# A third staging buffer for q and k, q's scale in its split, and a longer load in the planner of an attention and gated-MLP kernel

## The chip, the cores and the metric

The kernel runs on one core of a Trainium2 chip. The metric is the device time of one launch in microseconds (us): 979.78 us is the median of three runs of the kernel before (976.35 to 979.81). Traces are of one profiled execution; its span is 979.5 us.

The core has five engines with a queue each, which run in order and wait for one another by semaphores: TensorE (PE; its weight loads, PEld, are listed apart), VectorE (DVE), ScalarE (ACT), GpSimd (POOL) and SyncE (SP), which only issues DMAs here.

## The reference

Attention with rotary embedding over 8 batches x 8 heads, 576 positions, 64 features a head, and then a gated MLP on the heads put side by side (512 features). Cut to what matters:

```python
q_rot, k_rot = rotate(q), rotate(k)                # x1*cos - x2*sin, x1*sin + x2*cos
scores = scale * q_rot @ k_rot.T                   # scale = 1/sqrt(64) = 0.125
attn = softmax(scores)
x = (attn @ v).transpose(0, 2, 1, 3).reshape(8, 576, 512)
h = relu(x @ w_in);  u, v = halves of h            # 1024 -> 512 + 512
v_n = (v - mean(v)) / sqrt(var(v) + 1e-6)
v_s = einsum("ts,bsd->btd", w_spatial, v_n) + b_spatial
out = (u * v_s) @ w_out
```

## The kernel before, in words

**Tiling.** The 64 heads are worked off as 32 pairs, `i` = 0 to 31, four pairs a batch; a pair fills the 128 partitions. The two heads of a pair are called 0 and 1, and each has five row tiles of 128 (the last of 64) against all 576 keys: the score tiles (0,0) to (0,3), one tile (0,4) that both heads share, and (1,0) to (1,3), nine a pair. Behind the fourth pair of each batch stands that batch's MLP. Its matmuls are spread over the four pairs that come next.

**Precision.** Most matmuls run on operands that are split in two: a rounded part "hi" (made by ACT, `round_hi`, L309) and the remainder "lo" = x - hi (`rest_lo`, L312, on DVE or POOL). The products hi.hi, hi.lo and lo.hi are added up.

**Preparing a pair** (`prepare(i)`). Two tiles `st{i}_0` (q) and `st{i}_1` (k), each 128 x 1216 floats, are loaded with 576 KB each (all loads are issued by SyncE, L306). Each tile holds x and x with its halves swapped. Two products with the tables of cosines and sines (L401) and a sum (L405) make the rotation; for q the table is `tabq`, the table `tabs` times 0.125, made once by ACT (L465). Then ACT rounds q into the second half of its tile, q's remainder overwrites the sum (L312), ACT rounds k (L309, two instructions), and k's remainder goes to `lk`. Ten DMAs stack the parts into `qs0`, `qs1`, `ks0`, `ks1` and `qz`, of which there is one set: `ks1` is written again only when the last score tile of the pair before has read it. The slots of `st` come from the pool `stage`, which has two. They go back when the tile's last reader is done: for k these are `lk` and the DMAs to `ks1`.

**A pair's attention.** `scores`: matmuls into PSUM (L536; L546 for pair 0), row maximum (`nmx`, DVE L557), exponential (`e1`, `e2`, ACT L559). `values`: transposes into PSUM slots `tp` (PE L576), their rounding `eh` (ACT L587) and remainder `el` (DVE L312), the product with v (PE L600), an ACT copy `avt` (L617) and a DVE sum into `x32` (L615); then POOL multiplies with the inverse row sums (L710), and ACT and POOL split the result. Pairs 0 to 3 take a simpler path for the values.

**The MLP.** Products `pa` (L744), `pb` (L767, copied out of PSUM by ACT into `u`, L770), `pc` (L785), `pd` (L800, copied out by ACT into `ob`, L803). `tp`, `pa`, `pb`, `pc` and `pd` share three PSUM slots, pool `pm`. A copy out of `pb` or `pd` that comes late holds back the next transposes.

**What sets the order.** All instructions are handed to a list scheduler (`Program.run`), which plays the kernel through with costs and latencies of its own and gives each engine, when it is free, the ready instruction with the lowest key. What comes out is fixed: an engine's queue then runs in just that order on the chip. Its numbers are the costs (`op(DMA, 1640, ...)` for a load of q or k), `LATENCY` (1700 ns behind a DMA), `SLOTS` and the keys. An instruction with `port=True` isn't started by the scheduler while the other of DVE and POOL holds one such. `pair_op` lets the scheduler choose between DVE and POOL for keys under `EARLY` = 140 (up to pair 7) and takes POOL behind that. In the start-up (to about 147 us) DVE also decodes the 64-bit weights (L344 to L353).

Of the kernel before, what the change touches and what calls it, by code (L numbers as in the profile page):

```python
# [9 lines left out]
F32 = mybir.dt.float32  # L10
# [22 lines left out]
SLOTS = {  # L33
    "stage": 2, "lk": 1, "vraw": 2, "vs": 2, "e2": 4, "e1": 2, "eh": 7, "rb": 1, "x32": 1, "xg": 7, "m": 4,
    "small": 3, "nmx": 3, "rt": 2, "sc": 2, "pv": 1, "pm": 3,
# [63 lines left out]
class Op:  # L99
    def __init__(self, costs, key, f, new, port):  # L100
        self.costs, self.key, self.f, self.new, self.port = costs, key, f, new, port
        self.eng = None
        self.waits, self.after, self.bufs = 0, [], []


class Program:
# [4 lines left out]

    def op(self, eng, ns, key, f, r=(), w=(), new=(), port=False):
        return self.either({eng: ns}, key, lambda e: f(), r, w, new, port)

    def either(self, costs, key, f, r=(), w=(), new=(), port=True):

        o = Op(costs, key, f, new, port)
        before = dict.fromkeys(self.writer[t] for t in (*r, *w) if t in self.writer)
        for t in w:
            before.update(dict.fromkeys(self.readers.pop(t, ())))  # L120
        for t in r:
# [12 lines left out]
        self.ops.append(o)
        return o

    def run(self, make):
# [29 lines left out]
        while events:  # L167
# [55 lines left out]
def tile_attention_gated_mlp(  # L223
# [157 lines left out]
    def prepare(i):  # L381
# [13 lines left out]

        def lo_q(e):
            rest_lo(e, st[0][:, :S].bitcast(F32R), st[0][:, :S], hi(0))

        def rope(j, part, eng):
            cols = slice(S * part.start, S * part.stop)  # L400
            f = lambda e: e.tensor_tensor(out=st[j][:, cols], in0=st[j][:, cols], in1=(tabs if j else tabq)[:, cols], op=ALU.mult)  # L401
            pair_op(S * (part.stop - part.start), key - K_ROPE, f, first=eng, r=["tabs" if j else "tabq"], w=[(st[j], c) for c in range(part.start, part.stop)])

# [40 lines left out]
    def prepare_whole(i, b, hp, key):  # L444
# [13 lines left out]

        if i == 0:
            for part in range(2):  # L460
                cols = slice(S * part, S * part + S)
                op(DMA, 820, -70 + part, lambda part=part, cols=cols: load(k[:, cols], qk[b, hp, 1, :, part]), w=[(k, part)], new=[] if part else [k])
                op(DMA, 820, -70 + part, lambda part=part, cols=cols: load(tabs[:, cols], tab[:, part]), w=[("tabs", part)])
            op(DMA, 1640, -68, lambda: load(q.tile, qk[b, hp, 0].rearrange("p c n -> p (c n)")), w=[q], new=[q])
            op(ACT, 1053, -50, lambda: nc.scalar.activation(tabq, tabs, AF.Copy, scale=0.125), r=[("tabs", 0), ("tabs", 1)], w=["tabq", "tabs"])  # L465
            for part in range(2):
                op(DVE, 680, -60, lambda part=part: nc.vector.tensor_tensor(out=turn(k, part, slice(0, S)), in0=turn(k, part, slice(0, S)), in1=turn(tabs, part, slice(0, S)), op=ALU.mult), r=[("tabs", part)], w=[(k, part)], port=True)
            op(DVE, 830, -59, lambda: sum_k(nc.vector), r=[(k, 0), (k, 1)], w=[kf], new=[kf], port=True)
            for n, (c0, c1) in enumerate(((0, Q0), (Q0, S))):
                cols = slice(c0, c1)  # L470
                op(DVE, dve_ns(2 * (c1 - c0)), -58 + 2 * n, lambda cols=cols: nc.vector.scalar_tensor_tensor(out=c2(q.tile)[:, :, cols], in0=c2(q.tile)[:, :, cols], scalar=0.125, in1=c2(tabs)[:, :, cols], op0=ALU.mult, op1=ALU.mult), r=[q, ("tabs", 0), ("tabs", 1)], w=[(q, n)], port=True)
                op(DVE, dve_ns(c1 - c0), -57 + 2 * n, lambda cols=cols: nc.vector.tensor_tensor(out=turn(q, 0, cols), in0=turn(q, 0, cols), in1=turn(q, 1, cols), op=ALU.add), w=[(q, n)], port=True)
        else:
            for j, st in enumerate((q, k)):
                t = ("tabq", "tabs")[j]
                op(DMA, 1640, key - K_LOAD, lambda j=j, st=st: load(st.tile, qk[b, hp, j].rearrange("p c n -> p (c n)")), w=[(st, 0), (st, 1)], new=[st])
                for part in range(2):
                    pair_op(S, key - K_ROPE, lambda e, st=st, part=part, t=(tabq, tabs)[j]: e.tensor_tensor(out=turn(st, part, slice(0, S)), in0=turn(st, part, slice(0, S)), in1=turn(t, part, slice(0, S)), op=ALU.mult), r=[t], w=[(st, part)])
            pair_op(S, key - K_SUM, lambda e: e.tensor_tensor(out=q[:, :S], in0=q[:, :S], in1=q[:, S:], op=ALU.add), r=[(q, 1)], w=[(q, 0)])
            pair_op(S + TW, key - K_SUM, sum_k, pieces=2, r=[(k, 0), (k, 1)], w=[kf], new=[kf])  # L480
        op(DMA, 910, key - K_LOAD + 1, lambda: load(vr.tile, v[b, hp]), w=[vr], new=[vr])
# [452 lines left out]
```

## Time and profile before

| what | us |
|---|---|
| median of three runs | 979.78 (976.35 to 979.81) |
| span of the profiled execution | 979.5 |
| PE busy | 933.2 |
| ACT busy | 736.7 |
| DVE busy | 667.2 |
| POOL busy | 580.7 |
| wait for the first score matmul (L546) on q's products | 10.7 |

The page lists for each group of instructions its line, engine, what it writes and reads, count, busy time and the mean duration of one, and then the idle time of the engine ahead of it with what ended it. In a timeline the columns are start, length, engine, line, and in brackets the engine's idle time before and its releaser. The granted clock of TensorE is 1.00 in every window, so nothing here is a matter of clocks.

### The profile page before, as it was taken

The page shows a single profiled execution, that of the slowest core. Times are in us where ns is not written, and L with a number is a line of the kernel's source. Part 1 is how long each engine was busy: PE and PEld are TensorE (multiplying, and loading weights), DVE is VectorE, ACT ScalarE, POOL GpSimd, SP SyncE. Part 2 cuts the span into 40 slices and gives each one's busy share as a digit, 9 for nine tenths or more (in the row PEclk, how much of TensorE's full clock was granted, in tenths as well). Part 3 has the DMA queues.
Part 4 walks back from the last instruction along what each step waited for, and adds up shares of the span by engine and source line. Part 5 has one row for each costly group of instructions (what it writes and reads, how often), then busy time and mean ns, then how long its engine had stood idle before and what let it go on. Part 6 is the DMA issues. An engine that isn't in the chain of part 4 may idle for free.

```text
span 979.5 us, 19484 instructions
## 1 busy us (share of the span) xinstructions
PE 933.2 (95%) x6614; PEld 853.3 (87%) x6614; DVE 667.2 (68%) x1479; ACT 736.7 (75%) x1839; POOL 580.7 (59%) x505
## 2 busy tenths in 40 slices
PE   4988999999999999999999999999999999999998
PEld 2555689998899989999899988999889988999998
DVE  5899897766867577675776658676676756767331
ACT  4788798677976779776897768877797677976452
POOL 5566356656757656774756756666585765672121
PEclk9999999999999999999999999999999999999999
DMA  7776644454254554445444444445524455330101
GB/s 264 236 233 170 180 117 118 126 150 126 82 139 114 155 150 109 106 119 161 126 124 117 113 147 125 119 126 150 142 78 125 125 152 149 97 91 21 61 1 49
DMA packets 56181, 124.64 MB, mean 127 GB/s; under 512 B 13201, under 2 KB 13201, under 8 KB 56082
## 3 DMA queue, kind: packets, MB, share of 16 engines
q1 hardware_dynamic: 56082, 123.40, 45.7%
q8 instruction: 53, 0.87, 0.3%
q14 instruction: 46, 0.38, 0.1%
HBM read 66.03 MB, written 9.58 MB: 77 GB/s over the span
## 4 chain that ended last, share of the span: by engine, by line
PE 61%; ACT 13%; DMA 10%; DVE 7%; POOL 5%; issue 2%; SPq 2%; ACTq 0%; POOLq 0%; DVEq 0%
PE pc L785 12%; PE sc L536 10%; PE tp L576 9%; PE pv L600 9%; PE pd L800 7%; PE pb L767 6%; PE pa L744 4%; ACT e L559 4%; POOL st L401 3%; DMA st<-in_qk_dram 3%; DMA qs<-st 3%; DVE nmx L557 2%; SPq L306 2%; ACT eh L587 2%; ACT vv L827 2%
## 5 line engine op out<-in xcount | busy, mean ns | idle before, releaser
L587 ACT ACTIVATE eh<-tp 128x384 fp32r<-128x384 f32 (+1 forms) x504 | 217.5, 433 | 87.8 <-PE tp L576 70.6
L312 DVE TENSOR_TENSOR el<-tp,eh 128x384 fp32r<-128x384 f32 x336 | 185.8, 554 | 107.5 <-ACT eh L587 98.2
L559 ACT ACTIVATE e<-sc,nmx 128x576 f32<-128x576 f32 x288 | 213.0, 741 | 37.0 <-DVE nmx L557 34.1
L557 DVE TENSOR_REDUCE nmx<-sc 128x1 f32<-128x576 f32 x288 | 214.9, 748 | 31.9 <-PE sc L536 23.3
L576 PE MATMUL tp<-ident,e 128*128 128x128 f32 (+1 forms) x1176 | 196.9, 273 | 16.1 <-ACT ob L803 9.3
L401 POOL TENSOR_TENSOR st<-st,tabq 128x576 f32<-128x576 f32 x60 | 85.1, 1435 | 167.6 <-DMA st<-in_qk_dram 105.9
L576 PEld LDWEIGHTS tp<-ident,e 128*128 128x128 f32 (+1 forms) x1176 | 144.8, 138 | 34.2 <-ACT ob L803 10.7
L600 PE MATMUL pv<-eh,vs 128*128 128x384 f32 (+1 forms) x560 | 154.0, 316 | 0.2
L785 PE MATMUL pc<-wsp,vn 128*128 128x288 f32 x768 | 143.2, 303 | 0.5 <-DVE u L843 0.5
L767 PE MATMUL pb<-x,wi 128*128 128x288 f32 x768 | 141.3, 306 | 0.3 <-ACT u L770 0.3
L800 PE MATMUL pd<-g,wo 128*128 128x288 f32 x768 | 140.9, 304 | 0.0
L536 PE MATMUL sc<-ks,qs 128*128 128x288 f32 x620 | 133.1, 304 | 2.8 <-ACT e L559 2.2
L744 PE MATMUL pa<-wi,x 128*128 128x512 f32 x448 | 133.1, 407 | 1.3 <-DVE el L312 1.2
L536 PE MATMUL sc<-lk,qz 128*128 128x288 f32 x558 | 119.6, 296 | 0.0
L785 PEld LDWEIGHTS pc<-wsp,vn 128*128 128x128 f32 x768 | 114.9, 189 | 2.9 <-DVE u L843 0.9
L800 PEld LDWEIGHTS pd<-g,wo 128*128 128x128 f32 x768 | 113.7, 189 | 2.6
L767 PEld LDWEIGHTS pb<-x,wi 128*128 128x128 f32 x768 | 111.9, 189 | 3.3 <-PE pb L767 1.3
L600 PE MATMUL pv<-el,vs 128*64 128x384 f32 (+1 forms) x448 | 113.7, 294 | 0.0
L536 PEld LDWEIGHTS sc<-ks,qs 128*128 128x128 f32 x620 | 99.5, 189 | 13.5 <-ACT e L559 7.1
L312 DVE TENSOR_TENSOR eh<-tp,eh 64x256 fp32r<-64x256 f32 (+1 forms) x168 | 59.7, 356 | 65.2 <-ACT eh L587 56.8
L600 PEld LDWEIGHTS pv<-eh,vs 128*128 128x128 f32 x560 | 97.8, 188 | 5.6 <-DVE x L615 1.6
L710 POOL TENSOR_TENSOR x<-x,rb 128x576 f32<-128x576 f32 x31 | 44.3, 1430 | 93.9 <-DVE x L615 90.2
(173 smaller groups left out, 1536.4 us busy)
## 6 DMA issues: line engine op xcount, KB each, us to landing
st<-in_qk_dram SPq DMA_DIRECT2D x63, 576.0 KB
ks<-st SPq DMA_DIRECT2D x124, 160.0 KB
qs<-st SPq DMA_DIRECT2D x124, 144.0 KB
vr<-in_v_dram SPq DMA_DIRECT2D x32, 320.0 KB
out_dram<-ob SPq DMA_DIRECT2D x32, 288.0 KB
qz<-st SPq DMA_DIRECT2D x62, 144.0 KB
ws<-in_w_spT_dram SPq DMA_DIRECT2D x2, 576.0 KB
st<-in_qk_dram SPq DMA_DIRECT2D x2, 288.0 KB
```

The source lines that it names most:

```text
L312: eng.tensor_tensor(out=lo, in0=src, in1=hi.bitcast(F32), op=ALU.subtract)
L401: f = lambda e: e.tensor_tensor(out=st[j][:, cols], in0=st[j][:, cols], in1=(tabs if j else tabq)[:, cols], op=ALU.mult)
L536: nc.tensor.matmul(pt[:, c * 512:c * 512 + HALF], lhsT=lhsT, rhs=rhs[:, k0 + c * HALF:k0 + (c + 1) * HALF], start=(n == 0), stop=(n == len ...
L557: op(DVE, 665, key + K_MAX, lambda: nc.vector.tensor_reduce(out=nmx.tile, in_=tops(), op=ALU.max, axis=AX.XY, negate=True), r=[pt], w=[nmx ...
L559: op(ACT, 730, key + K_EXP, lambda: nc.scalar.activation(e[:, e0:e0 + S].rearrange("p (c n) -> p c n", c=2), tops(), AF.Exp, bias=nmx.tile ...
L576: nc.tensor.transpose(out=tp[:e.shape[1], m * P:m * P + P], in_=e, identity=ident)
L587: nc.scalar.activation(h, p, AF.Copy)
L600: nc.tensor.matmul(pv[0:rows, c1:c2], lhsT=vs[:, kt, h, vp, :], rhs=part[:, c1:c2], start=(kt == 0 and n == 0 and c1 == 0), stop=last)
L744: nc.tensor.matmul(pm.tile, lhsT=lhsT, rhs=win[1, d][:, j, :], start=(d == 0 and n == 0), stop=(d == 3 and n == len(todo) - 1))
L767: nc.tensor.matmul(pm[:, :HALF], lhsT=win[0, d][:, i, f * P:(f + 1) * P], rhs=x[d][:, at:at + HALF], start=(d == 0 and n == 0), stop=(d == ...
L785: nc.tensor.matmul(pm[:, :HALF], lhsT=lhsT, rhs=rhs, start=(t == 0 and n == 0), stop=(t == 4 and n == 1))
L800: nc.tensor.matmul(pm[:, :HALF], lhsT=wout[d,][:, i, m * P:(m + 1) * P], rhs=gs[d][:, at:at + HALF], start=(d == 0 and n == 0), stop=(d == ...
```

## The change

It has five parts. `stage` has three slots; the room comes from `tabq`, which is gone. q is multiplied with `tabs`, like k. q's scale is applied where q is split: ACT's rounding takes scale=0.125 (`hi_q`, L397 of the changed kernel), and the remainder is 0.125 x q - hi in one scalar-tensor-tensor (`lo_q`, L400), which is given to DVE, whereas POOL made most of the remainders before. The scheduler adds `LATE_LOAD` = 2200 ns to the time after which it takes a load of q or k as landed. And it counts 10 ns more for a POOL instruction. A branch of `prepare_whole` that is never run is dropped as well.

```diff
-    "stage": 2, "lk": 1, ...
+    "stage": 3, "lk": 1, ...
+LATE_LOAD = 2200
...
 def pool_ns(n):
-    return 150 + n * 32 // 15
+    return 160 + n * 32 // 15
...
-                    heapq.heappush(events, (now + chosen.costs[e] + LATENCY[e], n + 1, "done", chosen))
+                    heapq.heappush(events, (now + chosen.costs[e] + LATENCY[e] + chosen.late, n + 1, "done", chosen))
...
-    tabq = T([P, 2 * S], F32, "tabq")
...
-        def lo_q(e):
-            rest_lo(e, st[0][:, :S].bitcast(F32R), st[0][:, :S], hi(0))
+        def hi_q():
+            nc.scalar.activation(hi(0), st[0][:, :S], AF.Copy, scale=0.125)
+
+        def lo_q():
+            nc.vector.scalar_tensor_tensor(out=st[0][:, :S].bitcast(F32R), in0=st[0][:, :S], scalar=0.125, in1=hi(0).bitcast(F32), op0=ALU.mult, op1=ALU.subtract)
...
-            f = lambda e: e.tensor_tensor(out=st[j][:, cols], in0=st[j][:, cols], in1=(tabs if j else tabq)[:, cols], op=ALU.mult)
+            f = lambda e: e.tensor_tensor(out=st[j][:, cols], in0=st[j][:, cols], in1=tabs[:, cols], op=ALU.mult)
...
-            op(DMA, 1640, key - K_LOAD, lambda j=j: load(...), w=[(st[j], 0), (st[j], 1)], new=[st[j]])
+            op(DMA, 1640, key - K_LOAD, lambda j=j: load(...), w=[(st[j], 0), (st[j], 1)], new=[st[j]], late=LATE_LOAD)
...
-        op(ACT, 573, key - K_HIQ, lambda: round_hi(hi(0), st[0][:, :S]), r=[(st[0], 0)], w=[(st[0], 1)])
-        pair_op(S, key - K_LOQ, lo_q, r=[(st[0], 1)], w=[(st[0], 0)])
+        op(ACT, 573, key - K_HIQ, hi_q, r=[(st[0], 0)], w=[(st[0], 1)])
+        op(DVE, dve_ns(S), key - K_LOQ, lo_q, r=[(st[0], 1)], w=[(st[0], 0)], port=True)
...
-            op(ACT, 1053, -50, lambda: nc.scalar.activation(tabq, tabs, AF.Copy, scale=0.125), r=[("tabs", 0), ("tabs", 1)], w=["tabq", "tabs"])
```

Lines behind L475 of the kernel before stand seven lines higher in the changed one (L559 is L552, L803 is L796); the products are L404 and the sums L408 there. In the rows below a name is followed by the number of its allocation.

How the change moves instructions shows in three queues at one place, around the loads of pair 9. SyncE before, behind the stacking of pair 8:

```order
L306 DMA out_0_dram<-ob0_0_2684 128x576
L306 DMA st9_0_2807<-in_qk_dram 128x1152
L306 DMA st9_1_2831<-in_qk_dram 128x1152
L306 DMA rt7d_2799<-rt7_2800 9x32 x4
L306 DMA out_0_dram<-ob0_1_2792 128x576
L306 DMA rb7_2928<-rt7d_2799 64x576
```

and in the changed kernel:

```order
L306 DMA out_0_dram<-ob0_0_2686 128x576
L306 DMA st9_1_2801<-in_qk_dram 128x1152
L306 DMA rt7d_2791<-rt7_2792 9x32 x4
L306 DMA out_0_dram<-ob0_1_2807 128x576
L306 DMA st10_0_2877<-in_qk_dram 128x1152
L306 DMA rb7_2899<-rt7d_2791 64x576
```

The load of k of pair 9 stands at the place where the load of q of pair 9 stood, and that of q of pair 10 comes three rows behind it; q of pair 9 was loaded earlier, ahead of pair 8's stacking.

POOL before, from pair 9's products to the normalising of pair 7 (`x32_7`):

```order
L401 TENSOR_TENSOR st9_0_2807<-st9_0_2807,tabq_65 128x576 x2
L401 TENSOR_TENSOR st9_1_2831<-st9_1_2831,tabs_64 128x576
L405 TENSOR_TENSOR st9_0_2807<-st9_0_2807 128x576
L401 TENSOR_TENSOR st9_1_2831<-st9_1_2831,tabs_64 128x576
L312 TENSOR_TENSOR st9_0_2807<-st9_0_2807 128x576
L405 TENSOR_TENSOR st9_1_2831<-st9_1_2831 128x576
L710 TENSOR_TENSOR x32_7_2776<-x32_7_2776,rb7_2928 128x576
```

and in the changed kernel:

```order
L404 TENSOR_TENSOR st9_1_2801<-st9_1_2801,tabs_64 128x576 x2
L408 TENSOR_TENSOR st9_1_2801<-st9_1_2801 128x576
L404 TENSOR_TENSOR st10_0_2877<-st10_0_2877,tabs_64 128x576 x2
L408 TENSOR_TENSOR st10_0_2877<-st10_0_2877 128x576
L703 TENSOR_TENSOR x32_7_2766<-x32_7_2766,rb7_2899 128x576
```

k's two products and its sum stand first and no longer alternate with q's; q's of pair 10 follow. q's remainder (the L312 row) is gone from POOL.

ACT before, around the first rounding of pair 9 (`st9_0` is q, `st9_1` k; `pd0_20` and `pd0_21` are products of the first MLP that are copied to `ob0_2`):

```order
L803 ACTIVATE ob0_2_2895<-pd0_20_2849 128x288
L587 ACTIVATE eh7_2_2_2900<-tp7_2_2_2890 128x384
L617 ACTIVATE avt7_1_2906<-pv7_1_2794 64x384
L559 ACTIVATE e1_8_0_2917,sums0_68<-sc8_0_2_2880,nmx8_0_2_2888 128x576
L587 ACTIVATE eh7_2_3_2937<-tp7_2_3_2908 128x384
L309 ACTIVATE st9_0_2807<-st9_0_2807 128x576
L803 ACTIVATE ob0_2_2895<-pd0_21_2902 128x288
L559 ACTIVATE e2_8_1_2956,sums0_68<-sc8_0_3_2922,nmx8_0_3_2935 128x576
L587 ACTIVATE eh7_2_4_2970<-tp7_2_4_2958 64x2x128
```

and in the changed kernel:

```order
L796 ACTIVATE ob0_2_2903<-pd0_20_2856 128x288
L580 ACTIVATE eh7_2_2_2908<-tp7_2_2_2895 128x384
L610 ACTIVATE avt7_1_2914<-pv7_1_2781 64x384
L552 ACTIVATE e1_8_0_2925,sums0_67<-sc8_0_2_2885,nmx8_0_2_2893 128x576
L580 ACTIVATE eh7_2_3_2941<-tp7_2_3_2916 128x384
L552 ACTIVATE e2_8_1_2951,sums0_67<-sc8_0_3_2930,nmx8_0_3_2939 128x576
L796 ACTIVATE ob0_2_2903<-pd0_21_2910 128x288
L309 ACTIVATE st9_1_2801<-st9_1_2801 128x576
L309 ACTIVATE st9_1_2801<-st9_1_2801 128x64
L580 ACTIVATE eh7_2_4_2974<-tp7_2_4_2961 64x2x128
```

The first row of `st9` here is k's rounding now; `e2_8_1<-sc8_0_3` and the copy of `pd0_21`, which stood behind q's, stand ahead of it.

More of the change, by code (lines that the diff above doesn't have):

```diff
@@ L33 @@
 SLOTS = {
[L34 removed]
+    "stage": 3, "lk": 1, "vraw": 2, "vs": 2, "e2": 4, "e1": 2, "eh": 7, "rb": 1, "x32": 1, "xg": 7, "m": 4,
     "small": 3, "nmx": 3, "rt": 2, "sc": 2, "pv": 1, "pm": 3,
@@ L99, with __init__ @@
 class Op:
-    def __init__(self, costs, key, f, new, port):
+    def __init__(self, costs, key, f, new, port, late):
         self.costs, self.key, self.f, self.new, self.port = costs, key, f, new, port
-        self.eng = None
+        self.eng, self.late = None, late
         self.waits, self.after, self.bufs = 0, [], []
@@ L110, in __init__, with op, either @@
         self.ops, self.writer, self.readers = [], {}, {}
[L112 to L117, printed above, removed]
+    def op(self, eng, ns, key, f, r=(), w=(), new=(), port=False, late=0):
+        return self.either({eng: ns}, key, lambda e: f(), r, w, new, port, late)
+    def either(self, costs, key, f, r=(), w=(), new=(), port=True, late=0):
+        o = Op(costs, key, f, new, port, late)
         before = dict.fromkeys(self.writer[t] for t in (*r, *w) if t in self.writer)
@@ L394, in hi @@
             return st[j][rows, S:2 * S + TW * j].bitcast(F32R)
-        def lo_q(e):
-            rest_lo(e, st[0][:, :S].bitcast(F32R), st[0][:, :S], hi(0))
+        def hi_q():
+            nc.scalar.activation(hi(0), st[0][:, :S], AF.Copy, scale=0.125)
+        def lo_q():
+            nc.vector.scalar_tensor_tensor(out=st[0][:, :S].bitcast(F32R), in0=st[0][:, :S], scalar=0.125, in1=hi(0).bitcast(F32), op0=ALU.mult, op1=ALU.subtract)
         def rope(j, part, eng):
             cols = slice(S * part.start, S * part.stop)
-            f = lambda e: e.tensor_tensor(out=st[j][:, cols], in0=st[j][:, cols], in1=(tabs if j else tabq)[:, cols], op=ALU.mult)
-            pair_op(S * (part.stop - part.start), key - K_ROPE, f, first=eng, r=["tabs" if j else "tabq"], w=[(st[j], c) for c in range(part.start, part.stop)])
+            f = lambda e: e.tensor_tensor(out=st[j][:, cols], in0=st[j][:, cols], in1=tabs[:, cols], op=ALU.mult)
+            pair_op(S * (part.stop - part.start), key - K_ROPE, f, first=eng, r=["tabs"], w=[(st[j], c) for c in range(part.start, part.stop)])
         def rope_sum(j, eng):
@@ L408, in prepare @@
         for j in range(2):
-            op(DMA, 1640, key - K_LOAD, lambda j=j: load(st[j][:, :2 * S], qk[b, hp, j].rearrange("p c n -> p (c n)")), w=[(st[j], 0), (st[j], 1)], new=[st[j]])
+            op(DMA, 1640, key - K_LOAD, lambda j=j: load(st[j][:, :2 * S], qk[b, hp, j].rearrange("p c n -> p (c n)")), w=[(st[j], 0), (st[j], 1)], new=[st[j]], late=LATE_LOAD)
         op(DMA, 910, key - K_LOAD + 1, lambda: load(vr.tile, v[b, hp]), w=[vr], new=[vr])
@@ L457, in sum_k @@
             e.tensor_tensor(out=kf[:, :TW], in0=k[:, 4 * P:S], in1=k[:, S + 4 * P:], op=ALU.add)
[L459 to L480, printed above, removed]
@@ new lines, in prepare_whole @@
+        for part in range(2):
+            cols = slice(S * part, S * part + S)
+            op(DMA, 820, -70 + part, lambda part=part, cols=cols: load(k[:, cols], qk[b, hp, 1, :, part]), w=[(k, part)], new=[] if part else [k])
+            op(DMA, 820, -70 + part, lambda part=part, cols=cols: load(tabs[:, cols], tab[:, part]), w=[("tabs", part)])
+        op(DMA, 1640, -68, lambda: load(q.tile, qk[b, hp, 0].rearrange("p c n -> p (c n)")), w=[q], new=[q])
+        for part in range(2):
+            op(DVE, 680, -60, lambda part=part: nc.vector.tensor_tensor(out=turn(k, part, slice(0, S)), in0=turn(k, part, slice(0, S)), in1=turn(tabs, part, slice(0, S)), op=ALU.mult), r=[("tabs", part)], w=[(k, part)], port=True)
@@ new lines, in prepare_whole @@
+        op(DVE, 830, -59, lambda: sum_k(nc.vector), r=[(k, 0), (k, 1)], w=[kf], new=[kf], port=True)
+        for n, (c0, c1) in enumerate(((0, Q0), (Q0, S))):
+            cols = slice(c0, c1)
+            op(DVE, dve_ns(2 * (c1 - c0)), -58 + 2 * n, lambda cols=cols: nc.vector.scalar_tensor_tensor(out=c2(q.tile)[:, :, cols], in0=c2(q.tile)[:, :, cols], scalar=0.125, in1=c2(tabs)[:, :, cols], op0=ALU.mult, op1=ALU.mult), r=[q, ("tabs", 0), ("tabs", 1)], w=[(q, n)], port=True)
+            op(DVE, dve_ns(c1 - c0), -57 + 2 * n, lambda cols=cols: nc.vector.tensor_tensor(out=turn(q, 0, cols), in0=turn(q, 0, cols), in1=turn(q, 1, cols), op=ALU.add), w=[(q, n)], port=True)
```

## The prediction

> **What bounds the kernel now.** I read the page's busy shares and its 40 slices first, then the table of windows, then TensorE's waits from 147 to 906 us, and last the timeline around two of its stalls.
>
> ```profile
> PE 933.2 (95%) x6614; PEld 853.3 (87%) x6614; DVE 667.2 (68%) x1479; ACT 736.7 (75%) x1839; POOL 580.7 (59%) x505
> ...
> PE   4988999999999999999999999999999999999998
> ...
> DVE  5899897766867577675776658676676756767331
> ```
>
> ```profile
> 49.00:73.50 24.50, 19.84 (x132) 12.56 (x130) 23.63 (x41) 20.36 (x48) 15.04 (x13) 1.00 0.77 233
> 73.50:98.00 24.50, 21.20 (x141) 13.54 (x141) 23.88 (x45) 20.48 (x53) 15.68 (x14) 1.00 0.63 170
> ...
> 147.00:906.00 759.00, 743.30 (x5418) 704.70 (x5417) 522.59 (x1189) 596.76 (x1500) 483.37 (x411) 1.00 0.45 122
> ```
>
> The columns of the windows are length, then busy time of PE, PEld, DVE, ACT and POOL, the granted clock, and DMA. There are two regimes. Up to about 147 us VectorE is full (23.63 and 23.88 of 24.5 us) and TensorE is not. From 147 us on TensorE is full: 743.30 of 759 us, so 15.7 us are open, and only there does a shorter wait shorten the run one for one. TensorE's waits in that window are these:
>
> ```profile
> PE tp L576 <- ACT ob L803: 9.3, 6, 2.1
> PE tp L576 <- ACT u L770: 4.6, 4, 1.5
> PE pc L785 <- DVE u L843: 0.5, 1, 0.5
> ```
>
> Ten stalls, 9.3 + 4.6 = 13.9 us, are of one kind: a transpose (L576) waits for a PSUM slot that an ACT copy out of PSUM (`ob` or `u`) gives back late. The timeline around the stall at 226 us says why the copy is late.
>
> ```profile
> 213.24 2.48 SPq L306 DMA_DIRECT2D st<-in_qk_dram  x2
> ...
> 217.23 0.36 SPq L306 DMA_DIRECT2D out_dram<-ob  x1
> ```
>
> ```profile
> 219.39 2.81 POOL L401 TENSOR_TENSOR st<-st,tabq 128x576 f32<-128x576 f32 x2 [8.34 <-DMA rt7d<-rt]
> 222.16 1.42 POOL L401 TENSOR_TENSOR st<-st,tabs 128x576 f32<-128x576 f32 x1
> 223.54 1.40 POOL L405 TENSOR_TENSOR st<-st 128x576 f32<-128x576 f32 x1
> ```
>
> ```profile
> 224.97 0.68 ACT L309 ACTIVATE st<-st 128x576 fp32r<-128x576 f32 x1 [2.79 <-POOL st L405]
> 225.56 0.39 ACT L803 ACTIVATE ob<-pd 128x288 f32<-128x288 f32 x1
> 225.85 0.73 ACT L559 ACTIVATE e<-sc,nmx 128x576 f32<-128x576 f32 x1
> 226.48 0.20 ACT L559 ACTIVATION_READ_ACCUMULATOR e<-sc,nmx 128x1 f32 x1
> ```
>
> ```profile
> 226.01 0.55 PE L576 MATMUL tp<-ident,e 128*128 128x128 f32 x3 [1.95 <-ACT ob L803]
> ```
>
> SyncE issues the loads of pair 9 at 213.24. POOL starts to multiply q at 219.39, some 6 us later; the scheduler had counted 1640 + 1700 ns. q's sum ends at 224.94. ACT, in order, has stood for 2.79 us at q's rounding (L309) with `ob` queued behind it, and TensorE loses 1.95 us. At 285 us it is the same with `u` in place of `ob`: ACT waits 1.64, TensorE 1.47.
>
> ```profile
> 284.23 0.68 ACT L309 ACTIVATE st<-st 128x576 fp32r<-128x576 f32 x1 [1.64 <-POOL st L405]
> ```
>
> ```profile
> 285.26 0.55 PE L576 MATMUL tp<-ident,e 128*128 128x128 f32 x3 [1.47 <-ACT u L770]
> ```
>
> **The change, part by part.** The sum starts from the profiled execution itself, 979.5 us of span; the median of the three runs, 979.78, lies 0.3 above it, and the lowest, 976.35, 3.1 below.
>
> *Third buffer and longer load.* In the order shown above, q's load goes to SyncE one pair ahead: `st10_0` where `st9_0` stood. So q's rounding is never the late one again. But k's load keeps the place that q's had, because its slot is still given back by the k before it. k is what ACT can wait for next, and the stall goes only as far as k's rounding is better placed. Two numbers decide. First, readiness: q was ready after four POOL steps (219.39 to 224.94, one of them k's), k will be after three, two products and a sum: 2.81 + 1.40 = 4.2 us, so 1.4 us earlier. Second, the place in ACT's queue. In the order, the exponential of score (0,3) and the `ob` that was blocked stand ahead of pair 9's waiting instruction now. ACT does them in 0.83 (225.85 to 226.68) + 0.39 us, and both had their inputs by then. For pair 9 that leaves 2.79 - 1.4 - 1.2 = 0.2 us of wait, and the `ob` for which TensorE fell idle at 224.06 (226.01 - 1.95) is no longer behind it.
>
> For the other pairs I counted TensorE's work in the order, at its own spacing in the chain of waits:
>
> ```profile
> 226.91 0.40 PE pd L800 x3
> 227.31 0.81 PE sc L536 x6
> 228.11 0.40 PE pd L800 x3
> 228.51 0.33 PE tp L576 x3
> ```
>
> The count runs from the last score of pair i-2, which frees `ks1` and so the slot, to the last matmul whose result ACT takes ahead of the waiting rounding. Pairs with i mod 4 = 1 (the six `ob` stalls): 12.5 us before, 14.0 after, so 1.5 + 1.4 = 2.9 us in hand against waits of at most 2.79, the longest of the 24 in this row:
>
> ```profile
> ACT st L309 <- POOL st L405: 21.0, 24, 2.8
> ```
>
> Pairs with i mod 4 = 3 (the `u` stalls): 12.7 before and 12.9 after, so 1.6 in hand against waits of at most 1.64; pair 11 alone gets 0.4 less than before (12.3), so 1.0 in hand, and some 0.4 us of its 1.47 stays. Mod 0: 15.2 both times, 1.4 in hand against a wait of at most 1.03 that cost TensorE nothing:
>
> ```profile
> 315.64 0.69 ACT L309 ACTIVATE st<-st 128x576 fp32r<-128x576 f32 x1 [1.03 <-POOL st L405]
> ```
>
> Mod 2: 14.6 before, 12.8 after, the only place that gets worse, by 1.8 - 1.4 = 0.4; there q's sum was ready long before its rounding (pair 10: sum from 250.76, rounding at 255.72), so it has room.
>
> ```profile
> 250.76 1.43 POOL L405 TENSOR_TENSOR st<-st 128x576 f32<-128x576 f32 x1
> ```
>
> ```profile
> 255.72 0.70 ACT L309 ACTIVATE st<-st 128x576 fp32r<-128x576 f32 x1
> ```
>
> I take -13.9 + 0.4 for pair 11 + 0.6 for remainders of 0.1 to 0.2 at some of the others: **-12.9**. Ends: 0, if k waits as q did, and -13.9.
>
> *q's products moved ahead on POOL.* `st10_0`'s two products and sum (4.2 us) now stand between pair 9's k and `x32_7`. POOL was idle there until VectorE gave it `x`:
>
> ```profile
> 234.47 1.42 POOL L710 TENSOR_TENSOR x<-x,rb 128x576 f32<-128x576 f32 x1 [5.39 <-DVE x L615]
> ```
>
> So 4.2 us go into 5.39 us of idle time, and q's remainder has left this stretch as well (1.43 us). Its load is issued after `ob0_1`'s output, near 217.6, and lands near 223.6, when k's sum ends. It may be 6 us later before `x32_7` suffers. Cost: 0.
>
> *Remainder of q: from POOL to VectorE.* POOL loses 30 instructions of 1431 ns, VectorE gains 31. The new form has no row of its own. Nearest are a product of the same shape, 758 ns alone and 1296 ns next to POOL's, and a scalar-tensor-tensor of 768 elements:
>
> ```profile
> L312 POOL TENSOR_TENSOR st<-st 128x576 fp32r<-128x576 f32 x30 | 42.9, 1431 | 0.7 <-ACT st L309 0.7
> ```
>
> ```profile
> L401 DVE TENSOR_TENSOR st<-st,tabq 128x576 f32<-128x576 f32 x2 | 2.6, 1296 | 0.1
> ...
> L467 DVE TENSOR_TENSOR st<-st,tabs 128x576 f32<-128x576 f32 x2 | 1.5, 758 | 6.6 <-DMA tabs<-in_tab_dram 6.6
> ...
> L471 DVE SCALAR_TENSOR_TENSOR st<-st,tabs 128x768 f32<-128x768 f32 x1 | 1.0, 952 | 0.0
> ```
>
> 952 x 576/768 = 714, so I take 0.75 us each. Its cover is VectorE's waiting for ACT's rounded scores, 136 pieces of 0.72 us in the mean, and in the steady part only one 0.5 us wait of TensorE named VectorE (`u` L843, above). Cost there: 0. Without the cover it is 27 x 0.75 = 20 us.
>
> ```profile
> DVE el L312 <- ACT eh L587: 98.2, 136, 1.5
> ```
>
> The Trainium skill, in "SBUF — State Buffer", section "Who interferes with whom", speaks against this edit: a VectorE instruction with both inputs in SBUF and a GpSimd instruction that reads SBUF exclude each other, and the later one waits for the whole of the other. Here the 1296 beside the 758 ns agrees in direction, at 0.54 us, well under a whole 1431 ns POOL instruction; by the full lock a collision would cost up to 1.43 us.
>
> *Start-up, 0 to 147 us.* VectorE is the bound, so its work counts. Of pairs 1 to 5, eight products, sums and remainders of q and k stood on VectorE, with the remainder of pair 5's k; now three, and five remainders of q. At the means of rows like these
>
> ```profile
> L557 DVE TENSOR_REDUCE nmx<-sc 128x1 f32<-128x576 f32 x288 | 214.9, 748 | 31.9 <-PE sc L536 23.3
> ...
> L312 DVE TENSOR_TENSOR wo<-dcwo,wo 128x512 fp32r<-128x512 f32 x4 | 2.7, 684 | 0.1
> ```
>
> the work ahead of pair 3's last row maximum grows from 72.8 to 75.2 us, and ahead of pair 5's scores it is equal, 101.5 and 101.6. Against it, the load that stood on the chain of waits at 105 us is issued earlier:
>
> ```profile
> 105.24 5.54 DMA st<-in_qk_dram
> ```
>
> I take 0, with ends -4 (most of that 5.54) and +4 (2.4, and three remainders at 0.54 more).
>
> *tabq gone, cost numbers.* One ACT instruction of 1.16 us goes:
>
> ```profile
> L465 ACT ACTIVATE tabq<-tabs 128x1152 f32<-128x1152 f32 x1 | 1.2, 1163 | 5.3 <-DMA tabs<-in_tab_dram 5.3
> PE sc L546 <- DVE st L472: 10.7, 1, 10.7
> ```
>
> It lies in the first 11 us, where TensorE waits for VectorE's `st`: 0. The scaled rounding is the same ACT form: 0. The planner's numbers run on no engine.
>
> Sum: 979.5 - 12.9 + 0 = 966.6; with the 0.3 around the span, **967 us**.
>
> **Rivals.**
> 1. *k takes the stall over.* k's load is issued no earlier than q's was, so if the 1.4 us or the better places don't hold (say k's rounding is late by half of what q's was), half of 13.9 stays: 974. For it: the same slot chain, the same 6 us of load. Against: the count above.
> 2. *The gain is eaten behind it.* TensorE's queue is in order, and what follows the ten stalls may wait for the next late thing; then 978 to 980. Against: 743.30 of 759 us are busy and the ten stalls are all but 1.8 us of the rest.
> 3. *Start-up gets shorter* by the 4 us named: 963.
> 4. *Slower: the remainder on VectorE runs into POOL's reads.* Place: 27 remainders from pair 5 on, each ahead of an `el` that TensorE's values need. Price: 0.75 us plus x of waiting for the port, less 0.72 of cover, each: 27 x (0.03 + x). It eats the gain from x = 0.45, close to the 0.54 of the rows; at x = 1.0, between 0.54 and POOL's whole 1.43, it is +27.8, so 995. Against: TensorE hardly ever waits for VectorE now, and the scheduler keeps both off the port in its own clock. By the rule of "SBUF — State Buffer" in the Trainium skill, x could reach the whole 1.43 and the time 1006.
>
> **How the numbers follow.** Forecast 0.55, k takes over 0.18, eaten 0.10, shorter start-up 0.10, slower 0.07. A measurement of this kernel can tell about 0.5%, 4.9 us, so faster means under 974.9. Faster: 0.55 + 0.10 + 0.11 of rival 1 = 0.76. Same: 0.07 + 0.10 = 0.17. Slower: 0.07. The low end is 979.5 - 13.9 - 4 + 0.3 = 961.9, less 1 because one of before's own runs lay 3.1 us under the others: 961. The high end is 978, which takes in the +4 of start-up, rival 1 and the near half of rival 2; left out are rival 4 and the other half, 0.12.
>
> **What would show it.** The ten waits of the transposes for `ob` and `u` should fall from 13.9 to about 1 us, ACT's wait for POOL's sum (21.0 us in the page of waits) to under 6, and the window 147 to 906 should hold the same matmuls in about 746 us. If ACT waits at L309 for k, rival 1 is right. If the new VectorE rows read 1.3 us or more and TensorE's waits name `el`, rival 4 is. Start-up is read off the time at which pair 5's first scores begin. The prediction is wrong at its root if the stalls go and the span does not follow.

## The result, and the profile after

| | median, us | range | runs |
|---|---|---|---|
| before | 978.84 | 976.35 to 980.73 | 8 |
| changed | 972.96 | 972.02 to 975.07 | 8 |

The ratio is 0.9943 (95% interval 0.9929 to 0.9957): 5.9 us faster. The profiled execution of the changed kernel has a span of 971.5 us and took 973.27. Runs lie about 1.8 us above their spans, those of before too.

The page's busy shares, the waits of TensorE from 147 to 900 us, ACT's wait for POOL's sums, and two windows of the start-up:

```profile
PE 937.6 (97%) x6614; PEld 857.1 (88%) x6614; DVE 692.6 (71%) x1505; ACT 734.5 (76%) x1835; POOL 551.2 (57%) x482
```

```profile
PE pb L760 <- DVE el L312: 2.8, 3, 1.1
PE tp L569 <- DVE eh L312: 1.0, 2, 0.8
PE sc L529 <- ACT e L552: 0.6, 3, 0.2
PE pb L760 <- ACT u L763: 0.4, 1, 0.4
PE pb L760 <- DVE eh L312: 0.3, 1, 0.3
```

```profile
ACT st L309 <- POOL st L408: 0.9, 5, 0.2
```

```profile
49.00:73.50 24.50, 21.35 (x127) 14.66 (x128) 22.36 (x38) 20.10 (x49) 11.86 (x11) 0.91 0.81 239
73.50:98.00 24.50, 21.97 (x136) 14.17 (x135) 24.07 (x40) 18.94 (x47) 15.77 (x14) 0.95 0.60 178
```

The ten waits of the transposes for `ob` and `u` are gone, and ACT's wait went from 21.0 to 0.9 us. VectorE still fills the start-up (22.36 and 24.07 of 24.5 us), and the granted clock, 1.00 in every window of before, is 0.91 and 0.95 there. Pair 9 in POOL's and ACT's timelines: k's products and sum end at 226.07, its rounding comes at 227.18, behind the `ob`, with 1.1 us in hand.

```profile
221.75 2.81 POOL L404 TENSOR_TENSOR st<-st,tabs 128x576 f32<-128x576 f32 x2 [7.75 <-DMA st<-in_qk_dram]
224.64 1.43 POOL L408 TENSOR_TENSOR st<-st 128x576 f32<-128x576 f32 x1
```

```profile
226.89 0.40 ACT L796 ACTIVATE ob<-pd 128x288 f32<-128x288 f32 x1
227.18 0.83 ACT L309 ACTIVATE st<-st 128x576 fp32r<-128x576 f32 x2
```

**Where the time went.** The kernels have the same matmuls in different orders, so equal clock times are not equal work. I gave each matmul the 30th percentile of the spacing of its kind and shape over all traces here (859.1 us in all, the same for every kernel) and took TensorE's lag: the time at which it reaches a given amount of this work, less that work. **Start-up** below is the lag at 120 us of work, **steady** is what is added from there to the last matmul.

| kernel | median (its job's before) | ratio, 95% interval | start-up | steady |
|---|---|---|---|---|
| before, first profile | 978.84 | | 72.7 | 44.0 |
| changed, first profile | 972.96 (978.84) | 0.9943 (0.9929 to 0.9957) | 76.5 | 32.2 |
| r1_before | 979.46 (980.12) | 0.9992 (0.9968 to 1.0017) | 72.7 | 41.9 |
| r2_after | 972.61 (980.12) | 0.9908 (0.9872 to 0.9944) | 77.9 | 30.2 |
| e1_late0 | 991.94 (979.60) | 1.0139 (1.0106 to 1.0172) | 85.1 | 40.4 |
| e2_two_slots | 982.14 (979.60) | 1.0032 (1.0014 to 1.0049) | 83.4 | 33.1 |
| e4_late_from5 | 972.79 (979.60) | 0.9938 (0.9919 to 0.9957) | 74.7 | 31.6 |
| e5_before_late | 975.12 (979.60) | 0.9957 (0.9941 to 0.9973) | 76.3 | 32.8 |
| e3_lo_either | 977.70 (980.12) | 0.9974 (0.9947 to 1.0001) | 79.1 | 32.9 |
| e6_before_late5 | 969.24 (980.12) | 0.9872 (0.9830 to 0.9915) | 72.2 | 32.4 |
| f1_slots_lo_either | 980.55 (978.70) | 1.0013 (0.9996 to 1.0030) | 85.8 | 33.6 |
| f2_two_slots | 973.63 (978.70) | 0.9935 (0.9914 to 0.9957) | 75.7 | 34.0 |
| f3_late1100 | 968.69 (978.70) | 0.9888 (0.9864 to 0.9911) | 75.4 | 27.4 |
| f4_late4000 | 997.35 (978.70) | 1.0175 (1.0145 to 1.0205) | 75.7 | 57.1 |
| g1_pair1 | 973.01 (978.75) | 0.9941 (0.9920 to 0.9963) | 75.5 | 32.8 |
| g2_from2 | 976.35 (978.75) | 0.9982 (0.9969 to 0.9995) | 78.9 | 32.8 |
| g5_after_from2 | 981.06 (978.75) | 1.0023 (1.0006 to 1.0039) | 83.1 | 33.2 |
| g3_mixed | 965.40 (978.75) | 0.9870 (0.9854 to 0.9885) | 71.7 | 28.8 |

Each lag comes from one profiled execution, which can lie some us off the median (f1's took 984.0 us, its median is 980.55). 120 us of work is reached at about 193 us of the clock time, so "start-up" here goes on past the stretch that VectorE fills.

So the change won 11.8 us in the steady part and lost 3.9 at the start; together that is the 8.0 us between the spans. Two theories on the gain stood against each other, the longer load (L) and the third slot (S); on the loss, the longer load again, and q's remainder on VectorE.

### The profile page after: what moved, and what is told of

The parts are those of the page before. It is cut to its first block, busy times and chain, and to the rows that moved or that the text cites. A ratio compares the mean times of both kernels' runs of the same rounds, so it can differ in the third digit from the quotient of the medians.

```text
span 971.5 us, 19517 instructions
## 1 busy us (share of the span) xinstructions
PE 937.6 (97%) x6614; PEld 857.1 (88%) x6614; DVE 692.6 (71%) x1505; ACT 734.5 (76%) x1835; POOL 551.2 (57%) x482
## 4 chain that ended last, share of the span: by engine, by line
PE 76%; ACT 12%; DVE 5%; issue 2%; DMA 1%; SPq 0%; ACTq 0%; DVEq 0%
PE sc L529 13%; PE pc L778 12%; PE pv L593 12%; PE tp L569 11%; PE pd L793 11%; PE pb L760 9%; PE pa L737 7%; ACT e L552 4%; ACT eh L580 2%; ACT vv L820 1%; PE pv L666 1%; DVE nmx L550 1%; ACT vn L309 1%; ACT avt L610 1%; ACT st L309 1%
## 5 line engine op out<-in xcount | busy, mean ns | idle before, releaser
L312 DVE TENSOR_TENSOR el<-tp,eh 128x384 fp32r<-128x384 f32 x336 | 186.1, 554 | 79.3 <-ACT eh L580 70.3
L552 ACT ACTIVATE e<-sc,nmx 128x576 f32<-128x576 f32 x288 | 213.0, 740 | 33.8 <-DVE nmx L550 19.4
L404 POOL TENSOR_TENSOR st<-st,tabs 128x576 f32<-128x576 f32 x119 | 168.6, 1438 | 110.3 <-DMA st<-in_qk_dram 64.2
L312 DVE TENSOR_TENSOR eh<-tp,eh 64x256 fp32r<-64x256 f32 (+1 forms) x168 | 59.8, 356 | 47.1 <-ACT eh L580 35.3
```

Source lines behind the costliest of these rows:

```text
L312: eng.tensor_tensor(out=lo, in0=src, in1=hi.bitcast(F32), op=ALU.subtract)
L552: op(ACT, 730, key + K_EXP, lambda: nc.scalar.activation(e[:, e0:e0 + S].rearrange("p (c n) -> p c n", c=2), tops(), AF.Exp, bias=nmx.tile ...
```

## The experiments

**Which part makes the gain.** Each of these undoes one part of the change, or makes one alone.

```diff
-LATE_LOAD = 2200
+LATE_LOAD = 0
```

> The changed kernel with LATE_LOAD = 0: three slots, q's scale in its split and the remainder on VectorE stay, only the planner's longer load goes. Theory L (the planner's longer load removed the ten stalls of 13.9 us, by putting the roundings later in ACT's queue): they come back in good part, ACT again waits at the rounding for POOL's sum, and the time is 978 to 985 us. Theory S (the third slot removed them, because q is loaded a pair ahead): they stay away and the time stays at 973 or below. On the start-up, the changed kernel lost 3.8 us on TensorE's work in the first 150 us. If the longer load did that (it puts pair 1's scores behind pair 0's values), this kernel wins them back, 3 to 4 us in the window to 150 us; if VectorE's new remainder did it (1.63 and 1.69 us at 35 and 40 us instead of 0.75), it does not.

```diff
-    "stage": 3, "lk": 1, ...
+    "stage": 2, "lk": 1, ...
```

> The changed kernel with stage = 2: the longer load in the planner, the split and the remainder on VectorE stay, only the third slot goes. Theory L: the planner puts q's rounding late enough, the transposes' waits for ob and u stay under 3 us in all, and the time is 970 to 976 us. Theory S: q is loaded no earlier than before, its rounding is the late one again, the waits come back (over 8 us), and the time is 979 to 985 us.

The kernel before, with the longer load only:

```diff
+LATE_LOAD = 2200
...
-            op(DMA, 1640, key - K_LOAD, ..., new=[st[j]])
+            op(DMA, 1640, key - K_LOAD, ..., new=[st[j]], late=LATE_LOAD)
```

> The kernel before with the longer load in the planner alone: two slots, tabq, q's remainder on POOL. Theory L: the ten stalls go, by 10 us or more in the steady part, and the time is 968 to 974 us. Theory S: they stay for the most part and the time is 976 to 981 us. On the start-up: if the longer load alone costs it, TensorE is 3 to 4 us later at 150 us than in the kernel before; if the remainder on VectorE did it, it is level.

TensorE's waits behind 150 us, first e1_late0, then e2_two_slots:

```profile
PE tp L569 <- DVE el L312: 3.7, 6, 1.6
PE pb L760 <- DVE el L312: 3.2, 7, 0.5
PE pb L760 <- DVE eh L312: 2.5, 7, 0.4
...
PE tp L569 <- ACT u L763: 0.4, 1, 0.4
```

```profile
PE pd L793 <- DVE el L312: 1.4, 5, 0.3
PE pb L760 <- DVE sm L812: 1.2, 1, 1.2
PE sc L529 <- ACT e L552: 1.0, 6, 0.2
```

For the steady part theory L holds: with the longer load alone it is 32.8, with two slots 33.1, with three slots and no longer load 40.4. For the stalls themselves theory S was right in e1: the third slot by itself also takes the waits for `ob` and `u` away (0.4 us left), where L had them come back, but others of 9.4 us for VectorE's `el` and `eh` stand in their place. The times decide nothing here, because the start-up moved by up to 12 us, which none of the theories had: e1 and e5 missed both ranges, and e2's 982.14 us lies in the range of theory S though its stalls stayed away, as L said.

**How sure the parts are.** Both kernels once more:

> The kernel before once more, for a second profile. Its first profile has a span of 979.5 us, and the runs lie 1.8 us above their spans, so that execution took 981.3 us, above all eight that were timed beside the change (median 978.84). Theory N (the excess is start-up, where loads land at other times in each execution): a profile nearer the median is 1 to 4 us shorter, all of it in the first 150 us, and the ten stalls are 13 to 14.5 us again. Theory Q (the stalls themselves vary): the difference lies behind 150 us, and the stalls are 11 to 12 us.

> The changed kernel once more, for a second profile and more times. The steady part (from 150 us on) should take within 1 us of the first profile, with the same two 1.1 us waits at the maximum of the v half (a VectorE instruction of 1.69 us instead of 0.41). The start-up may differ by up to 2 us. The median should be 972 to 974 us.

```profile
PE tp L576 <- ACT ob L803: 9.0, 6, 2.1
PE tp L576 <- ACT u L770: 2.5, 3, 1.3
PE pc L785 <- DVE u L843: 0.5, 1, 0.5
```

That is r1_before behind 150 us. Theory Q is right, not N: the start-up is the same to 0.1 us, and the stalls are 11.5 us instead of 13.9. The first profile of before was an execution of 981.3 us (979.5 + 1.8), above all eight timed beside it; against r1_before its span is 2.1 us longer, and its stalls 2.4. r2_after has a steady part 2.0 us shorter than the first profile and lacks the two waits of 1.1 us that I expected there again; its start-up is 1.4 longer. Differences of the start-up under 1.5 us, and of the steady part under 2, are therefore not told apart here.

**What costs the start-up.** The longer load from pair 5 on only, in the changed kernel and in the kernel before:

```diff
-new=[st[j]], late=LATE_LOAD)
+new=[st[j]], late=LATE_LOAD * (i >= 5))
```

> The changed kernel with the longer load counted only from pair 5 on, so the start-up is planned with the short load and the rest with the long one. If the longer load cost the 3.8 us at the start, TensorE is back at the times of before at 150 us and the time is 968 to 970 us. If the remainder on VectorE did, or the queue of five products on POOL at 10.9 us, the start stays as it is and the time is 972 to 974 us.

> The kernel before with the longer load counted from pair 5 on and nothing else: two slots, tabq, remainder on POOL. The first pairs are ordered as in the kernel before. If the steady gain is the longer load's alone (10.0 us in the trace with the longer load everywhere) and it costs about 3 us at the start, this gives the gain without the cost: start-up level with the kernel before, the ten stalls gone, the time 967 to 970 us. If the start-up varies on its own and the longer load has no part in it, the time is that of the longer load everywhere, 973 to 976 us.

q's remainder as in the kernel before, with the scale in the shared table:

```diff
+op(ACT, 1053, -50, lambda: nc.scalar.activation(tabs, tabs, AF.Copy, scale=0.125 ** 0.5), w=["tabs", ("tabs", 0), ("tabs", 1)])
...
-            nc.scalar.activation(hi(0), st[0][:, :S], AF.Copy, scale=0.125)
+            round_hi(hi(0), st[0][:, :S])
...
-        op(DVE, dve_ns(S), key - K_LOQ, lo_q, r=[(st[0], 1)], w=[(st[0], 0)], port=True)
+        pair_op(S, key - K_LOQ, lo_q, r=[(st[0], 1)], w=[(st[0], 0)])
```

> The changed kernel with q's scale moved once more: the table is multiplied by the root of 0.125 in place (so q and k both carry it), q's rounding and remainder are plain again, and the remainder may go to POOL as in the kernel before. Three slots and the longer load stay. Theory V (the remainder on VectorE costs the start-up, by 31 instructions of which two took 1.63 and 1.69 us there): the start-up is 2 to 4 us shorter than in the changed kernel, the time 969 to 971 us. Theory W (the longer load orders pair 1 late, whoever makes the remainder): the start-up is as long as in the changed kernel, the time 972 to 975 us.

e6 came out as expected: start-up level with the kernel before, gain kept, 969.24 us. Against e5 it says that the longer load for pairs 1 to 4 alone costs 4.0 us there. e3 speaks against theory V: with the remainder off VectorE the start-up is not 2 to 4 us shorter but longer still, 79.1. It is not a clean test, since its edit also puts a scaling of the table ahead of pair 1's products (POOL starts them at 11.42 instead of 10.91 us). In the changed kernel the short early load leaves 2.0 us of the loss in e4's profile, and e4's median does not differ from the changed kernel's: the profile is of one of the three executions with a granted clock of 1.00 throughout (970.3 to 972.2 us), and the other seven, at a mean of 0.996 to 0.998, took 972.6 to 976.2. For that rest, f1 is e3 and f2 is e2 with the longer load from pair 5 on:

> Three slots and the longer load from pair 5 on, with the table scaled in place and q's remainder free to go to POOL: beside the kernel before with the longer load from pair 5 on (969.24 us, start-up level with the kernel before) only the third slot and the table differ. Theory 3 (it is the third slot that costs the start-up the 2.5 us that are left with the short load there): TensorE is 2 to 3 us behind the kernel before at 120 us of its own work, and the time is 971 to 973 us. Theory 4 (it is the remainder on VectorE): it is level, and the time is 968 to 970 us.

> The changed kernel with two slots and the longer load from pair 5 on: beside the kernel before with the longer load from pair 5 on, only the split (scaled rounding, remainder on VectorE, no tabq) and 10 ns a POOL instruction in the planner differ. Theory 3: start-up level with the kernel before, the time 968 to 970 us. Theory 4: TensorE 2 to 3 us behind at 120 us of its own work, the time 971 to 973 us. In the steady part both expect the ten stalls gone without the third slot.

Neither theory holds. f2 (split, two slots) is 3.0 us late, f1 (three slots, plain remainder) 13.1, both together (e4) 2.0: the parts don't add. Last, whether it is pair 1's place. In the first two, the kernel before, and in the third, the changed one, the edit is the condition on `i`:

```diff
-late=LATE_LOAD * (i >= 5))
+late=LATE_LOAD * (i == 1 or i >= 5))
```

> The kernel before with the longer load counted for pair 1 and for pairs 5 to 31. Beside it stand two results: counted from pair 5 on (969.24 us, TensorE 72.2 us behind its own work at 120 us of it) and counted everywhere (975.12 us, 76.2 us behind). Theory 1 (pair 1 is the place: its scores are ordered later on TensorE, which then has nothing to put into pair 0's waits): as everywhere, 973 to 976 us and 75 to 77 us behind. Theory 2 (it is pairs 2 to 4, or any reshuffle of a stretch that VectorE fills): 968 to 972 us, or another start-up altogether.

```diff
-late=LATE_LOAD * (i >= 5))
+late=LATE_LOAD * (i >= 2))
```

> The kernel before with the longer load counted from pair 2 on, so pair 1 keeps its place. Theory 1: start-up level with the kernel before, 72 to 73 us behind at 120 us of work, 968 to 970 us. Theory 2: 74 us or more behind, 971 to 976 us.

> The changed kernel with the longer load counted from pair 2 on: pair 1's first scores move on TensorE from the 49th row of the order to the 24th. Theory 1: at 20 us of its own work TensorE is level with the kernel before (36 us) where the changed kernel is 3.4 to 3.9 us late, and 2 us or more of that are kept at 120 us: 969 to 971 us. Theory 2: what is won at 20 us is lost again by 120 us of work, and the time is 972 us or more.

Pair 1 late costs 2.8 us (g1), the number of theory 1 but not its place: at 20 us of work TensorE is 33.9 us behind there, ahead of the 36.0 of before, and loses the time later. Pair 1 in its old place and pairs 2 to 4 late costs 6.2 (g2), and in the changed kernel 10.4 (g5), though TensorE there too is 33.9 us behind at 20 us of work. Theory 2 stands: any new order of pairs 1 to 4 lengthened the start-up, by 2.0 to 13.1 us. Nor are these pairs the only place: kernels that differ from before only in the load counted from pair 5 on moved it by -0.9 to +3.0 (e6, and f3, f4 and g3_mixed below).

**How long a load to count.** In the kernel before, from pair 5 on:

```diff
-LATE_LOAD = 2200
+LATE_LOAD = 1100
```

> The kernel before with half the extra load time, 1100 instead of 2200 ns, from pair 5 on. If the number works because it brings the planner's load (1640 + 1700 + 2200 = 5540 ns) up to what the trace shows from issue to first product (some 6 us), half of it leaves ACT waiting at the rounding for part of the 1.1 us that are missing: 2 to 6 us of the stalls stay, and the time is 971 to 975 us. If any later place will do, it is 969 us again.

```diff
-LATE_LOAD = 2200
+LATE_LOAD = 4000
```

> The kernel before with 4000 ns from pair 5 on, more than the trace shows. If the planner only has to be late enough, the roundings have slack and the time is 968 to 970 us. If too late a rounding moves the wait on to the stacking of q and k and the first scores of the next pair, TensorE waits there, and the time is 971 us or more.

```diff
-late=LATE_LOAD * (i >= 5))
+late=LATE_LOAD if 5 <= i < 8 else LATE_LOAD // 2 if i >= 8 else 0)
```

> A version put together from what the runs showed: the kernel before with no extra load time for pairs 1 to 4, 2200 ns for pairs 5 to 7 and 1100 ns from pair 8 on. The start-up should be that of 2200 from pair 5 on (72.2 us behind at 120 us of work) and the steady part that of 1100 (27.4 us more by the end, against 32.4 with 2200 and 43.7 before): 963 to 966 us. If the gain of 1100 over 2200 comes from the pairs 5 to 7 alone, or the order shifts as a whole, it is 968 us or more.

TensorE's waits behind 150 us in f3, with ACT's wait, and then in f4:

```profile
PE pb L768 <- DVE el L313: 0.6, 1, 0.6
PE pc L786 <- DVE u L844: 0.5, 1, 0.5
```

```profile
ACT st L310 <- POOL st L406: 10.7, 14, 1.2
```

```profile
PE sc L537 <- DMA ks<-st: 10.9, 6, 3.2
PE tp L577 <- ACT u L771: 6.7, 6, 1.1
```

In the steady part half the number is better than all of it, 27.4 against 32.4; the start-up is 3.2 us longer, and the times are the same (968.69 and 969.24). ACT still waits 10.7 us at the roundings, but TensorE's waits come to 1.1 us, so little that it needs is behind them. The reading that the number has to match the trace's 6 us is refuted. 4000 ns shows the other end: the roundings come so late that the first scores wait for the stacking of k, 10.9 us in six pieces. g3_mixed joins e6's start-up with most of f3's steady part: **965.40 us, ratio 0.9870 (0.9854 to 0.9885)**, shorter than both kernels, with two slots and `tabq` as before. Its profile's span is 4.0 us shorter than e6's (963.4 and 967.4), but each measured against its own job's before they are level (0.9870 and 0.9872), so the gain over e6 is not shown on the times. The 10 ns more for a POOL instruction was not tried alone.

## Why the prediction was off

The forecast was 967 us, a gain of about 12; measured were 972.96 and a gain of 5.9. By its steps:

- **The bound and the stalls: right.** The ten stalls hung on the rounding in ACT's queue, and they went. The term was -12.9, measured -11.8 (32.2 - 44.0); with the second profiles it is between -9.7 and -13.8. Pair 9 should keep 0.2 us of wait at k's rounding and kept none. What came in their place is VectorE's, 4.1 us of waits for `el` and `eh` (1.9 in r2_after), which the 1.0 us that the term left for waits did not hold; so much of rival 2 came. Rivals 1 and 3 did not.
- **Which edit does it: not told apart.** I let the third slot and the longer load stand as one step. The longer load alone gives 32.4 to 32.8, so q's load a pair ahead added nothing that stands clear of the 2 us between two profiles of one kernel.
- **The remainder on VectorE in the steady part: right.** Cost 0; 32.2 and 30.2 with it, 32.4 and 32.8 without it. Rival 4 did not come.
- **The start-up: the step that failed.** I took 0, with ends of -4 and +4, from the VectorE work ahead of two landmarks (72.8 against 75.2 us, then 101.5 against 101.6). Measured are +3.9 and +5.2. VectorE was full only from 49 to 98 us, which the rows on either side of those that I read show (its busy time is the third):

```profile
24.50:49.00 24.50, 23.26 (x135) 14.10 (x133) 20.06 (x34) 18.67 (x48) 14.64 (x12) 1.00 0.78 236
98.00:122.50 24.50, 22.59 (x137) 15.08 (x137) 20.88 (x31) 17.82 (x45) 9.68 (x9) 1.00 0.67 180
```

Its busy time up to pair 3's last row maximum (its 36th) grew by 5.3 us in the traces (83.5 to 88.8), not 2.4; three remainders that took 1.22 to 1.69 us instead of 0.75 are 2.3 of that. And a sum of work says nothing of the waits inside it, nor does the sign that I had named: pair 5's first scores begin earlier, at 121.3 instead of 123.2 us, while TensorE is behind on its work. The first scores of pair 1 moved from 29.85 to 40.45 us, first before, then changed:

```profile
29.85 0.83 PE L536 MATMUL sc<-ks,qs 128*128 128x288 f32 x2
```

```profile
40.45 0.52 PE L529 MATMUL sc<-ks,qs 128*128 128x288 f32 x2
```

As I read it, TensorE then had nothing to put into pair 0's waits, and q's remainder added one of its own. The changed kernel's VectorE, POOL and TensorE at 35 us:

```profile
35.02 1.63 DVE L400 SCALAR_TENSOR_TENSOR st<-st 128x576 fp32r<-128x576 f32 x1
...
36.70 0.51 DVE L637 COPY et_3a<-tp_3a 128x384 f32<-128x384 f32 x1
```

```profile
34.63 3.29 POOL L312 TENSOR_TENSOR wsp<-ws,wsp 128x576 fp32r<-128x576 f32 x2
```

```profile
37.27 0.55 PE L628 MATMUL tp_3b<-ident,e 128*128 128x128 f32 x3 [1.11 <-DVE et_3a L637]
```

At 20 us of its work TensorE is 39.8 us behind instead of 36.0, and at 120 us 76.5 instead of 72.7. Shown is that planning pairs 1 to 4 with the longer load costs 4.0 us in the kernel before (e5 against e6); without it the changed kernel's profile is 1.8 to 3.2 us better at the start (e4), though its median is not. Which single instruction does it, is open: g5 and e4 win back what is lost at 20 us of work and pay at another place, and f3 and f4 lose about 3 us with pairs 1 to 4 untouched. The granted clock, which I took as 1.00 throughout, has a share in it that the last section bounds.
- **Around the span: mis-sized.** I took 0.3 us from a profile of one execution and the median of others. It is 1.8.

With the measured terms the sum closes: 979.5 - 11.8 + 3.9 + 1.8 = 973.4, against 973.27 for the profiled execution. The gain over the median, 5.9, is smaller than the 8.0 between the profiles, because the sum started from an execution of 981.3 us, 2.5 above the median of before; its stalls were long.

## What to carry to other kernels

Where a list scheduler writes the order, ask of its numbers whether they put an instruction that waits ahead of one that others wait for; try the number at half and at double, since too late can cost more than too early (a steady part of 57.1 with 4000 ns, 44.0 with none, 27.4 with 1100). Apply such a number only to the stretch whose stalls were read: here the same edit that gained some 10 us in the steady part lost 4 in a start-up bound by another engine. Predict a reordered start-up with wide ends, or keep its order.

## What the runs showed of the hardware

**VectorE and POOL block each other, for up to nearly a whole instruction.** q's remainder took 757 ns in the median and up to 1694 (first two rows: shortest, median, longest). A maximum of VectorE with a single input (L810), 410 ns in the median, took 1.69 us from the moment a POOL product of 1.43 us had started, and TensorE lost 1.13 us for the `el` behind it:

```profile
L400 DVE SCALAR_TENSOR_TENSOR st<-st x31: 740/757/1694, 35.0 to 842.4; 128x576 fp32r<-128x576 f32 x31
```

```profile
L810 DVE TENSOR_SCALAR vv<-vv x8: 407/410/1689, 147.2 to 931.4; 64x512 f32<-64x512 f32 x8
```

```profile
378.02 1.69 DVE L810 TENSOR_SCALAR vv<-vv 64x512 f32<-64x512 f32 x1
```

```profile
378.00 1.43 POOL L703 TENSOR_TENSOR x<-x,rb 128x576 f32<-128x576 f32 x1 [0.60 <-PE tp L569]
```

```profile
380.35 0.66 PE L760 MATMUL pb<-x,wi 128*128 128x288 f32 x3 [1.13 <-DVE el L312]
```

The Trainium skill, "SBUF — State Buffer", section "Who interferes with whom", says that these two engines lock a shared pair of ports for a whole instruction, and names `tensor_scalar` among what can take it; the trace agrees, 1.69 - 0.41 = 1.28 us. Of the eight maxima two took 1.69 us. It goes the other way too: at 492.73 us the same two again start 0.02 us apart, and now the maximum takes its 0.41 us and the POOL product 1.73 instead of 1.43:

```profile
492.73 1.73 POOL L703 TENSOR_TENSOR x<-x,rb 128x576 f32<-128x576 f32 x1 [0.60 <-PE tp L569]
```

```profile
492.75 0.41 DVE L810 TENSOR_SCALAR vv<-vv 64x512 f32<-64x512 f32 x1
```

For q's remainder a collision cost somewhat less than what was left of the POOL instruction: at 39.57 us 1.08 us were left and it took 0.94 longer, at 89.47 us 0.61 and 0.46. Of the 31 remainders 8 were held up, by 0.61 us in the mean, close to the 0.54 that I had read. Five of the 8 lie in the steady part, whose length shows no cost of it.

**The granted clock halves for 3.41 us at a time, also without a long pause.** In the changed kernel TensorE paused for 1.19 us, and soon after the clock was 0.50 from 51.93 to 55.34 us:

```profile
50.19 0.53 PE L529 MATMUL sc<-ks,qs 128*128 128x288 f32 x2 [1.19 <-ACT e L552]
```

```profile
52.00:53.00 1.00, 1.00 (x7) 0.99 (x6) 1.00 (x3) 0.98 (x2) 0.13 (x1) 0.50 0.91 225
53.00:54.00 1.00, 0.84 (x4) 0.44 (x3) 0.67 (x2) 1.00 (x3) 0.62 (x1) 0.50 0.85 242
```

Up to 900 us the traces hold 19 such stretches, each 3.41 us long or two to five times that. In the 3.41 us ahead of each TensorE was busy for 59% of the time or less. A pause alone does not do it: in e2_two_slots one of 4.25 us passes at a granted clock of 1.00.

```profile
33.47 0.90 PE L628 MATMUL tp_0b<-ident,e 128*128 128x128 f32 x3 [4.25 <-DVE wi L312]
```

```profile
24.50:49.00 24.50, 19.10 (x90) 10.80 (x89) 20.64 (x36) 16.27 (x36) 13.43 (x12) 1.00 0.93 277
```

Some of the runs with long start-ups have the half clock for longer; e1_late0:

```profile
98.00:122.50 24.50, 14.95 (x66) 10.18 (x62) 20.22 (x33) 11.61 (x26) 7.07 (x5) 0.71 0.41 119
```

"TensorE: Matmul & The Clock Gate" in the Trainium skill, section "What's actually happening", lets the clock fall after an idle window of about 3.4 us. The pause ahead of the stretch at 51.93 was a third of that, so a stretch with little work suffices, or the window is read otherwise; no run here settles which.

At half clock a stretch can cost at most half its length, and that bounds the clock's share of the start-up loss. The changed kernel's profile has 6.8 us at 0.50, so at most 3.4 of its 3.9 us; its second profile has 3.4 us, so at most 1.7 of 5.2; e2_two_slots has none and is 10.7 us late. In f1_slots_lo_either 27.3 us at 0.50 could make up all of its 13.1. So the clock is not the cause of every loss, and its exact share stays open. Of the 4.0 us between e5 and e6 at most 1.7 are the clock's. Executions of the kernel before differ in it too, though its two profiles show 1.00: of 76 timed beside the experiments, the 30 with a mean clock of 1.000 have a median of 977.56 us, the 42 at 0.996 to 0.998 one of 980.29; whether the clock makes that difference or goes with it is not shown.
